# Attention and two feed-forward layers on one core: ScalarE's parametric rectifier carries the sign of a converted weight

## The chip, the cores and the metric

One core of a Trainium2 chip. The metric is device time in microseconds (us); less is better. The engines are TensorE (PE in the rows, its weight loads PEld), VectorE (DVE), ScalarE (ACT), GpSimd (POOL) and SyncE (SP), which here issues the DMAs.

## The reference

Three blocks follow each other, with 2304 tokens of width 512:

```python
# attention: 4 batches, 8 heads, 576 positions, head width 64
scores = q @ k.T / sqrt(64)     # heads 0-3: window of 32; heads 4-7: every 4th of 128 positions
attn = softmax(where(mask, scores, -1e9)) @ v
# first layer, w_in 512x2048, w_out 2048x512
h = x @ w_in
g = (a0 + a1*h + a2*h**2 + a3*h**3) / (1 + |b0|*|h| + |b1|*h**2 + 1e-6)
x = g @ w_out
# second layer, the same sizes
h = x @ w_in
out = (max(h, 0) + alpha * min(h, 0)) @ w_out
```

All four weight matrices reach the chip as 64-bit floats; everything else is 32-bit.

## The kernel before

**Conversion of the weights.** A weight arrives in chunks of 128x512 64-bit floats, seen as pairs of 32-bit words. `w_convert` makes 32-bit floats of two chunks at a time (a 128x1024 tile). The high word holds the sign, eleven bits of exponent and twenty of mantissa. ScalarE reads it as a 32-bit float, takes its absolute value and scales it by 2^-112, which moves the exponent so that its top bits are gone (L377, two instructions of 128x512). VectorE shifts the result left by three bits (L383, one instruction of 128x1024), which pushes them out and makes room for three more mantissa bits. It then ORs in the top three bits of the low word (L393, two instructions of 128x512), and last the sign bit of the high word (L398, two more). For five chunk pairs of the first layer's `w_out`, those in the table `SIGNED`, another way is taken: ScalarE makes the three low bits in place, with a copy on strided 16-bit words (L380, two instructions), and VectorE ORs sign and low bits in together (L386, two instructions). So VectorE has five instructions for a pair outside the table and three for one in it, and ScalarE two and four.

There are 32 such pairs, 16 in each layer. Those of the first layer are converted in the first part of the kernel, where they are also needed first. Of the second layer's, eleven are converted between the first layer's work (`w_early`), stored to DRAM and read back later, and five of `w_out` at the start of the second layer.

**The work on tokens.** `J` counts 48 steps of the first layer; each takes two 128-wide chunks of the hidden width for 384 tokens. A step is an in-projection on TensorE (`inproj`, L618, into the tile `ps_h`, which has two buffers), the rational function on ScalarE and VectorE (`rat_1`, `rat_2`, L636 to L650; L639 is the last instruction that reads a `ps_h` and so the one that frees it), and an out-projection (`outproj1`, L668), which TensorE does two steps later. In the first eight steps the operands are plain 32-bit floats. From the ninth on, each operand is a high and a low part (type fp32r) and each product three matmuls. For that `w_split` makes two parts of every converted weight (L418 on ScalarE, L419 on VectorE), and `g_split` of every result (L657, L658). Every second step also has the scores of an attention unit (L472, L482), its softmax (L494 to L539), its product with v (L553) and the copies of it that the next in-projections read (L583, L588). In this document a pair is two steps with one such unit. The second layer takes its in-projection in seven products of sums (L809) and its out-projection from L687.

**The order of the work.** TensorE, VectorE and ScalarE each run their instructions in the order in which they stand. `in_order_of_need` writes that order at the end of the build: it goes through the recorded instructions with a cost for each and what each depends on, and lets the one with the longest chain behind it go first. It fixes the order of those that it places in its first 197 us (`ORDERED`); behind that the order is that of the tile framework. SyncE's queue has the DMAs in one order: loads of raw weights (L350, L358), of attention (L445, L446), stores of converted weights (L362).

Of the kernel before, what the change touches and what calls it, by code (L numbers as in the profile page):

```python
# [7 lines left out]
F32 = mybir.dt.float32  # L8
# [3 lines left out]
U16 = mybir.dt.uint16  # L12
AF = mybir.ActivationFunctionType
ALU = mybir.AluOpType
# [16 lines left out]
W_BIAS = 2.0 ** -112  # L31
# [9 lines left out]
QW = UB // 2 * HEADS * QB  # L41
KW = UB // 2 * HEADS * CELL
ORDERED = 197e3
SIGNED = (('out', 4), ('out', 6), ('out', 8), ('out', 10), ('out', 12))
WARM = 8
SLOW = 6500
ORDER = "capaaawwwwwwawwwwwwwwa"
# [228 lines left out]
def attn_rational_prelu_kernel(  # L276
# [15 lines left out]
    nc = tc.nc  # L292
    scale = 1.0 / float(D) ** 0.5
# [37 lines left out]
    wt, raw_t, w32_t = {}, {}, {}  # L331
# [21 lines left out]
    def w_early(layer, kind, c):  # L353


        for i in range(2):
            t = rawp.tile([128, 2 * DM], U32, tag="raw", name="raw")
            nc.sync.dma_start(out=t, in_=src[layer, kind][c + i].bitcast(U32))  # L358
            raw_t[layer, kind, c + i] = t
        a = w_convert(layer, kind, c, f"outl{NC - 2}")  # L360
        w_dram[layer, kind, c] = dp.tile([128, 2 * DM], F32, name=f"w_dram_{kind}{c}")
        nc.sync.dma_start(out=w_dram[layer, kind, c], in_=a.bitcast(F32))  # L362

    def w_convert(layer, kind, c, tag=None):


        if layer == 1 or tag:
            a = wp.tile([128, 2 * DM], U32, tag=tag or f"{kind}l{c}", name=f"w{kind}{c}")
        else:
            a = rawp.tile([128, 2 * DM], U32, tag="u", name="u", bufs=1)  # L370
        signed = layer == 1 and (kind, c) in SIGNED
        halves = [slice(i * DM, (i + 1) * DM) for i in range(2)]
        raw = [raw_t.pop((layer, kind, c + i)) for i in range(2)]
        words = [t.rearrange("p (f t) -> p t f", t=2) for t in raw]
        for i in range(2):
            w32_t[layer, kind, c + i] = a[:, halves[i]]
            nc.scalar.activation(out=a[:, halves[i]].bitcast(F32), in_=words[i][:, 1, :].bitcast(F32), func=AF.Abs, scale=W_BIAS)  # L377
            if signed:
                quarters = raw[i].bitcast(U16).rearrange("p (f t) -> p t f", t=4)
                nc.scalar.activation(  # L380
                    out=quarters[:, 2, :], in_=quarters[:, 1, :], func=AF.Copy, scale=2.0 ** -13, bias=-8191.0 / 16384
                )
        nc.vector.tensor_scalar(out=a, in0=a, scalar1=3, scalar2=0, op0=ALU.logical_shift_left, op1=ALU.bitwise_or)  # L383
        if signed:
            for i in range(2):
                nc.vector.scalar_tensor_tensor(  # L386
                    out=a[:, halves[i]], in0=words[i][:, 1, :], scalar=0x80000007, in1=a[:, halves[i]],
                    op0=ALU.bitwise_and, op1=ALU.bitwise_or,
                )
            raw_t[layer, kind, c] = a  # L390
            return a
        for i in range(2):
            nc.vector.scalar_tensor_tensor(  # L393
                out=a[:, halves[i]], in0=words[i][:, 0, :], scalar=29, in1=a[:, halves[i]],
                op0=ALU.logical_shift_right, op1=ALU.bitwise_or,
            )
        for i in range(2):
            nc.vector.scalar_tensor_tensor(  # L398
                out=a[:, halves[i]], in0=words[i][:, 1, :], scalar=0x80000000, in1=a[:, halves[i]],
                op0=ALU.bitwise_and, op1=ALU.bitwise_or,  # L400
            )
        raw_t[layer, kind, c] = a
        return a
# [512 lines left out]
    def w_next(layer):  # L916
        for key in to_convert[layer][:1]:
            while (*key[:2], key[2] + 1) in to_load[layer]:
                w_loads(layer, 1)
            if key not in w_dram:  # L920
                w_convert(*key)
            if layer == 2:
                w_split(*key)
        del to_convert[layer][:1]
# [252 lines left out]
```

## Time and profile before

| | |
|---|---|
| median of three runs | 889.0 us (888.59 to 892.02) |
| the profiled execution | 889.99 us, of which 887.6 us are its span, from the first to the last instruction |
| TensorE | 862.5 us busy, 97% of the span |
| weight loads of TensorE | 765.5 us, 86% |
| VectorE | 761.9 us, 86% |
| ScalarE | 579.5 us, 65% |
| granted clock of TensorE | 0.996 of full speed on average |
| DMA | 90.48 MB, 102 GB/s on average |

The shares are averages over stages that have different limits, and a busy TensorE counts matmuls that overlap, so they are read stage by stage: the first 46 us are the first attention units and the first weights, the first layer ends near 500 us, and the second fills the rest.

### The profile page before, as it was taken

The numbers are of one execution on the slowest core, as the hardware profiler recorded it, in microseconds if no ns is written. First come the engines' busy times: TensorE is split into PE (matmuls) and PEld (weight loads), VectorE is DVE, ScalarE is ACT, GpSimd is POOL, SyncE is SP. The second block draws the span as 40 slices with busy tenths as digits, with TensorE's granted clock in tenths as the row PEclk, the third lists the DMA queues.
The fourth block names the chain that finished last, engine by engine and source line by source line (L and its number), as shares of the span: only waits on it lengthen the run. The fifth ranks groups of instructions, "written<-read, shape, count | busy, mean of one in ns | idle before, by whom it ended". The sixth has DMA issues, their size and how long they took to land.

```text
span 887.6 us, 17356 instructions
## 1 busy us (share of the span) xinstructions
PE 862.5 (97%) x7031; PEld 765.5 (86%) x7032; DVE 761.9 (86%) x1235; ACT 579.5 (65%) x1165; POOL 0.2 (0%) x4
## 2 busy tenths in 40 slices
PE   7899999999999999999999999999999999999998
PEld 5555578889999999898999999898888989899896
DVE  3899999999999899999999999998987678767642
ACT  4699977578777777777677665657554455644423
POOL 0000000000000000000000000000000000000000
PEclk9899999999999999999999999999999999999999
DMA  9956102123333434443021242323220011210001
GB/s 334 356 189 246 38 22 93 38 86 129 130 128 117 159 110 127 163 147 108 18 78 43 76 150 95 119 64 132 87 98 24 25 48 60 95 48 24 1 0 72
DMA packets 32911, 90.48 MB, mean 102 GB/s; under 512 B 3904, under 2 KB 11456, under 8 KB 32832
## 3 DMA queue, kind: packets, MB, share of 16 engines
q1 hardware_dynamic: 32832, 89.38, 29.1%
q8 instruction: 55, 0.90, 0.4%
q14 instruction: 24, 0.20, 0.1%
HBM read 74.17 MB, written 15.20 MB: 101 GB/s over the span
## 4 chain that ended last, share of the span: by engine, by line
PE 61%; DVE 19%; ACT 13%; DMA 4%; issue 2%; SPq 0%; ACTq 0%
PE ps_h L809 19%; PE ps_y L687 14%; PE ps_h L618 9%; PE ps_y L668 9%; PE ps_aS L687 4%; PE ps_aP L687 4%; DVE tc L649 2%; DVE tb L648 2%; ACT p L511 2%; DVE tb L645 2%; ACT tc L637 2%; DVE tc L650 2%; ACT p L526 2%; DVE tc L638 2%; DVE tc L639 2%
## 5 line engine op out<-in xcount | busy, mean ns | idle before, releaser
L618 PE MATMUL ps_h<-xh,winh 128*128 128x384 f32 x320 | 110.2, 344 | 6.8 <-DVE tc L639 6.8
L668 PE MATMUL ps_y<-gh,wouth 128*128 128x384 f32 x320 | 108.0, 338 | 0.0
L668 PE MATMUL ps_y<-gl,wouth 128*128 128x384 f32 x320 | 107.3, 335 | 0.0
L668 PE MATMUL ps_y<-gh,woutl 128*128 128x384 f32 x320 | 107.2, 335 | 0.0
L618 PE MATMUL ps_h<-xh,winl 128*128 128x384 f32 x320 | 107.1, 335 | 0.0
L618 PE MATMUL ps_h<-xl,winh 128*128 128x384 f32 x320 | 107.0, 334 | 0.0
L687 PE MATMUL ps_y<-wouth,gl 128*128 128x512 f32 x192 | 74.9, 390 | 0.0
L687 PE MATMUL ps_y<-woutl,gh 128*128 128x512 f32 x192 | 74.9, 390 | 0.0
L687 PE MATMUL ps_y<-wouth,gh 128*128 128x512 f32 x192 | 74.8, 390 | 0.0
L636 ACT ACTIVATE ta<-ps_h,root 128x384 f32<-128x384 f32 x96 | 56.2, 586 | 26.9 <-PE ps_h L618 22.8
L618 PEld LDWEIGHTS ps_h<-xh,winh 128*128 128x128 f32 x320 | 60.0, 188 | 12.1 <-DVE tc L639 10.5
L637 ACT ACTIVATE tc<-ps_h,co 128x384 f32<-128x384 f32 x96 | 65.3, 680 | 1.4 <-DVE gl L658 1.4
L657 ACT ACTIVATE gh<-tc 128x768 fp32r<-128x768 f32 x40 | 34.1, 851 | 44.2 <-DVE tc L650 44.1
L668 PEld LDWEIGHTS ps_y<-gh,wouth 128*128 128x128 f32 x320 | 60.0, 188 | 0.4
L716 DVE TENSOR_TENSOR gl<-tc,gh 128x768 fp32r<-128x768 f32 x48 | 45.8, 954 | 16.8 <-ACT gh L715 16.7
L715 ACT ACTIVATE gh<-tc 128x768 fp32r<-128x768 f32 x48 | 40.4, 841 | 30.5 <-PE ps_aP L687 28.0
L618 PEld LDWEIGHTS ps_h<-xl,winh 128*128 128x128 f32 x320 | 60.1, 188 | 0.1
L668 PEld LDWEIGHTS ps_y<-gl,wouth 128*128 128x128 f32 x320 | 60.1, 188 | 0.1
L668 PEld LDWEIGHTS ps_y<-gh,woutl 128*128 128x128 f32 x320 | 60.1, 188 | 0.1
L618 PEld LDWEIGHTS ps_h<-xh,winl 128*128 128x128 f32 x320 | 60.1, 188 | 0.0
L715 ACT ACTIVATE st_a<-w 128x1024 fp32r<-128x1024 f32 x24 | 25.5, 1062 | 50.4 <-PE ps_h L809 41.7
L639 DVE SCALAR_TENSOR_TENSOR tc<-tc,co,ps_h 128x384 f32<-128x384 f32 x96 | 58.0, 607 | 0.2
(203 smaller groups left out, 2287.7 us busy)
## 6 DMA issues: line engine op xcount, KB each, us to landing
w<-w_dram_in SPq DMA_DIRECT2D x24, 512.0 KB, 3.3
raw<-in_w_in_dram SPq DMA_DIRECT2D x16, 512.0 KB, 5.2
raw_inh<-in_w_out_dram SPq DMA_DIRECT2D x13, 512.0 KB, 3.4
y_dram<-os SPq DMA_DIRECT2D x24, 192.0 KB, 1.9
out_dram<-os SPq DMA_DIRECT2D x18, 256.0 KB, 2.1
ld_qk<-in_qv_d_dram SPq DMA_DIRECT2D x10, 448.0 KB, 3.5
ld_qk<-in_qv_p_dram SPq DMA_DIRECT2D x10, 416.0 KB, 3.7
raw_inh<-in_w_in_dram SPq DMA_DIRECT2D x8, 512.0 KB, 8.8
```

What stands on the lines that cost most here:

```text
L511: nc.scalar.activation(out=a["p"][:, j * CELL:(j + 1) * CELL], in_=a["s"][p][:, jj * CELL:(jj + 1) * CELL], func=AF.Exp, scale=scale, bias ...
L526: nc.scalar.activation(out=pv, in_=pv, func=AF.Copy, scale=a["rd"][:, j:j + 1])
L618: nc.tensor.matmul(out=hp[:, :BLK], lhsT=w, rhs=x, start=(k == 0), stop=(k == len(pairs) - 1))
L636: nc.scalar.activation(out=ta, in_=hp, func=AF.Abs, scale=root)
L637: nc.scalar.activation(out=tc_, in_=hp, func=AF.Identity, scale=co[:, 3:4], bias=co[:, 2:3])
L639: nc.vector.scalar_tensor_tensor(out=tc_, in0=tc_, scalar=co[:, 1:2], in1=hp, op0=ALU.add, op1=ALU.mult)
L657: nc.scalar.activation(out=hi, in_=g, func=AF.Copy)
L668: nc.tensor.matmul(out=yt[:, :BLK], lhsT=w[:, m * 128:(m + 1) * 128], rhs=g, start=(c == 0 and i == 0), stop=(c == NC - 1 and i == len(pai ...
L687: nc.tensor.matmul(out=yt, lhsT=g[:, tok], rhs=w, start=(first and i == 0), stop=(last and i == 2))
L715: nc.scalar.activation(out=hi, in_=t, func=AF.Copy)
L716: nc.vector.tensor_tensor(out=lo, in0=t, in1=hi.bitcast(F32), op=ALU.subtract)
L809: nc.tensor.matmul(out=hp, lhsT=u[:, ws], rhs=x[:, xs], start=(k == 0), stop=(k == 5))
```

## The change

`w_convert` no longer takes the absolute value. ScalarE's function at this place is the parametric rectifier (`Prelu`), with the scale as before and a slope for negative numbers of -2^32. A positive high word comes out as before. A negative one is made positive too, and 2^32 times as large, so that bit 5 of its exponent field is set; the shift by three that follows puts this bit at the place of the sign. The instructions that ORed in the sign (L398) go, and the table `SIGNED` with its branch (L380, L386). All 32 pairs now have two instructions on ScalarE and three on VectorE.

```diff
--- before.py
+++ after.py
@@ -41,7 +41,7 @@
 QW = UB // 2 * HEADS * QB
 KW = UB // 2 * HEADS * CELL
 ORDERED = 197e3
-SIGNED = (('out', 4), ('out', 6), ('out', 8), ('out', 10), ('out', 12))
+SIGN = -(2.0 ** 32)
 WARM = 8
 SLOW = 6500
 ORDER = "capaaawwwwwwawwwwwwwwa"
@@ -368,36 +368,19 @@
             a = wp.tile([128, 2 * DM], U32, tag=tag or f"{kind}l{c}", name=f"w{kind}{c}")
         else:
             a = rawp.tile([128, 2 * DM], U32, tag="u", name="u", bufs=1)
-        signed = layer == 1 and (kind, c) in SIGNED
         halves = [slice(i * DM, (i + 1) * DM) for i in range(2)]
         raw = [raw_t.pop((layer, kind, c + i)) for i in range(2)]
         words = [t.rearrange("p (f t) -> p t f", t=2) for t in raw]
         for i in range(2):
             w32_t[layer, kind, c + i] = a[:, halves[i]]
-            nc.scalar.activation(out=a[:, halves[i]].bitcast(F32), in_=words[i][:, 1, :].bitcast(F32), func=AF.Abs, scale=W_BIAS)
-            if signed:
-                quarters = raw[i].bitcast(U16).rearrange("p (f t) -> p t f", t=4)
-                nc.scalar.activation(
-                    out=quarters[:, 2, :], in_=quarters[:, 1, :], func=AF.Copy, scale=2.0 ** -13, bias=-8191.0 / 16384
-                )
+            nc.scalar.activation(
+                out=a[:, halves[i]].bitcast(F32), in_=words[i][:, 1, :].bitcast(F32), func=AF.Prelu, scale=W_BIAS, alpha=SIGN
+            )
         nc.vector.tensor_scalar(out=a, in0=a, scalar1=3, scalar2=0, op0=ALU.logical_shift_left, op1=ALU.bitwise_or)
-        if signed:
-            for i in range(2):
-                nc.vector.scalar_tensor_tensor(
-                    out=a[:, halves[i]], in0=words[i][:, 1, :], scalar=0x80000007, in1=a[:, halves[i]],
-                    op0=ALU.bitwise_and, op1=ALU.bitwise_or,
-                )
-            raw_t[layer, kind, c] = a
-            return a
         for i in range(2):
             nc.vector.scalar_tensor_tensor(
                 out=a[:, halves[i]], in0=words[i][:, 0, :], scalar=29, in1=a[:, halves[i]],
                 op0=ALU.logical_shift_right, op1=ALU.bitwise_or,
-            )
-        for i in range(2):
-            nc.vector.scalar_tensor_tensor(
-                out=a[:, halves[i]], in0=words[i][:, 1, :], scalar=0x80000000, in1=a[:, halves[i]],
-                op0=ALU.bitwise_and, op1=ALU.bitwise_or,
             )
         raw_t[layer, kind, c] = a
         return a
```

The lines behind `w_convert` stand 17 lower in the changed kernel (L639 becomes L622, L494 becomes L477). `in_order_of_need` is not edited, but it has other instructions to place, so the order on each engine moves too. Three places follow.

On VectorE, the first step of the first layer: `win` and `wout` are the tiles of converted weights with buffer numbers (`win_465` is the second pair), L638 and L639 the rational function on `ps_h`. Before:

```order
L498 TENSOR_SCALAR nm<-mx 128x6
L398 SCALAR_TENSOR_TENSOR win_465<-raw_outh_153,win_465 128x512
L638 TENSOR_TENSOR tc<-tc,ps_h 128x384
L393 SCALAR_TENSOR_TENSOR wout_569<-raw_inh_155,wout_569 128x512
L639 SCALAR_TENSOR_TENSOR tc<-tc,co,ps_h 128x384
L393 SCALAR_TENSOR_TENSOR wout_569<-raw_outh_157,wout_569 128x512
L519 TENSOR_SCALAR sm<-sm 128x6
L645 SCALAR_TENSOR_TENSOR tb<-ta,ratio 128x768
L520 RECIPROCAL rd<-sm 128x6
L638 TENSOR_TENSOR tc<-tc,ps_h 128x384
L383 TENSOR_SCALAR win_577<-win_577 128x1024
L639 SCALAR_TENSOR_TENSOR tc<-tc,co,ps_h 128x384
```

The same place of the changed kernel:

```order
L381 SCALAR_TENSOR_TENSOR wout_565<-raw_outh_157,wout_565 128x512
L477 TENSOR_REDUCE mx<-ps_aS 128x3
L477 TENSOR_REDUCE mx<-ps_aP 128x3
L621 TENSOR_TENSOR tc<-tc,ps_h 128x384
L481 TENSOR_SCALAR nm<-mx 128x6
L622 SCALAR_TENSOR_TENSOR tc<-tc,co,ps_h 128x384
L502 TENSOR_SCALAR sm<-sm 128x6
L503 RECIPROCAL rd<-sm 128x6
L628 SCALAR_TENSOR_TENSOR tb<-ta,ratio 128x768
L522 STREAM_TRANSPOSE pts<-p 128x384
L621 TENSOR_TENSOR tc<-tc,ps_h 128x384
L622 SCALAR_TENSOR_TENSOR tc<-tc,co,ps_h 128x384
```

The first `wout` is now whole before the step begins, and no conversion stands between L621 and L622 (before: L638 and L639).

On ScalarE, the stage in which the first layer's weights are converted, from a copy of an attention unit (L583) on. Before:

```order
L583 ACTIVATE xh_788<-ps_aS 128x192
L583 ACTIVATE xh_788<-ps_aP 128x192
L380 ACTIVATE raw_inh_175<-raw_inh_175 128x512
L380 ACTIVATE raw_outh_177<-raw_outh_177 128x512
L377 ACTIVATE win_1005<-raw_inh_877 128x512
L377 ACTIVATE win_1005<-raw_outh_879 128x512
L377 ACTIVATE wout_927<-raw_inh_776 128x512
L377 ACTIVATE wout_927<-raw_outh_778 128x512
L380 ACTIVATE raw_inh_776<-raw_inh_776 128x512
L380 ACTIVATE raw_outh_778<-raw_outh_778 128x512
L636 ACTIVATE ta<-ps_h,root 128x384
L637 ACTIVATE tc<-ps_h,co 128x384
```

The changed kernel there:

```order
L566 ACTIVATE xh_778<-ps_aS 128x192
L566 ACTIVATE xh_778<-ps_aP 128x192
L376 ACTIVATE win_987<-raw_inh_863 128x512
L376 ACTIVATE win_987<-raw_outh_865 128x512
L376 ACTIVATE wout_911<-raw_inh_766 128x512
L376 ACTIVATE wout_911<-raw_outh_768 128x512
L376 ACTIVATE wout_993<-raw_inh_867 128x512
L376 ACTIVATE wout_993<-raw_outh_869 128x512
L376 ACTIVATE win_1125<-raw_inh_960 128x512
L376 ACTIVATE win_1125<-raw_outh_962 128x512
L629 ACTIVATE ta<-tb,c1t 128x768
L619 ACTIVATE ta<-ps_h,root 128x384
```

The four copies of 16-bit words are gone, and two more pairs are converted in their place.

On VectorE, a conversion of `w_early` (the third pair of the second layer's `w_out`) between two steps, with buffer numbers, of which those of `ps_h` tell the in-projections apart. Before:

```order
L638 TENSOR_TENSOR tc_4069<-tc_4069,ps_h_4083 128x384
L519 TENSOR_SCALAR sm_4097<-sm_4097 128x6
L398 SCALAR_TENSOR_TENSOR wout4_4331<-raw_4327,wout4_4331 128x512
L639 SCALAR_TENSOR_TENSOR tc_4069<-tc_4069,co_109,ps_h_4083 128x384
L520 RECIPROCAL rd_4112<-sm_4097 128x6
L648 SCALAR_TENSOR_TENSOR tb_4068<-tb_4068,ta_4067 128x768
L649 SCALAR_TENSOR_TENSOR tc_4069<-tc_4069,co_109,ta_4067 128x768
L539 STREAM_TRANSPOSE pts_4127<-p_4096 128x384
L650 SCALAR_TENSOR_TENSOR tc_4069<-tb_4068,tc_4069 128x768
L638 TENSOR_TENSOR tc_4159<-tc_4159,ps_h_4160 128x384
L398 SCALAR_TENSOR_TENSOR wout4_4331<-raw_4329,wout4_4331 128x512
L639 SCALAR_TENSOR_TENSOR tc_4159<-tc_4159,co_109,ps_h_4160 128x384
```

The changed kernel, the last two instructions of the same conversion:

```order
L381 SCALAR_TENSOR_TENSOR wout4_4289<-raw_4285,wout4_4289 128x512
L481 TENSOR_SCALAR nm_4009<-mx_4008 128x6
L641 TENSOR_TENSOR gl_4199<-tc_3847,gh_4198 128x768
L621 TENSOR_TENSOR tc_4027<-tc_4027,ps_h_4028 128x384
L381 SCALAR_TENSOR_TENSOR wout4_4289<-raw_4287,wout4_4289 128x512
L622 SCALAR_TENSOR_TENSOR tc_4027<-tc_4027,co_109,ps_h_4028 128x384
L502 TENSOR_SCALAR sm_4055<-sm_4055 128x6
L503 RECIPROCAL rd_4070<-sm_4055 128x6
L628 SCALAR_TENSOR_TENSOR tb_4026<-ta_4025,ratio_111 128x768
L621 TENSOR_TENSOR tc_4027<-tc_4027,ps_h_4041 128x384
L622 SCALAR_TENSOR_TENSOR tc_4027<-tc_4027,co_109,ps_h_4041 128x384
```

Where a sign instruction stood in front of L639 twice, no instruction of the conversion is left; the conversion ends one step earlier.

## Rows read from the trace of the kernel before

**Rows 1.** Busy time by stage: start:end, length, then each engine's busy us (instructions).

```profile
core 0: us, PE busy (x) PEld busy (x) DVE busy (x) ACT busy (x) POOL busy (x), PEclk, DMA share, GB/s
27.70:46.41 18.71, 15.81 (x200) 8.56 (x197) 15.88 (x32) 14.23 (x40) 0.00 (x0) 0.89 0.88 341
46.41:127.87 81.46, 80.77 (x728) 49.62 (x728) 79.84 (x140) 76.95 (x167) 0.00 (x0) 1.00 0.36 126
127.87:190.92 63.05, 59.02 (x643) 53.64 (x637) 60.13 (x94) 42.06 (x107) 0.00 (x0) 1.00 0.18 57
190.92:209.67 18.75, 18.75 (x215) 18.11 (x209) 18.48 (x32) 14.03 (x36) 0.00 (x0) 1.00 0.27 93
209.67:406.54 196.87, 191.54 (x2186) 182.39 (x2181) 183.82 (x313) 149.50 (x375) 0.00 (x0) 1.00 0.41 136
500.36:610.00 109.64, 109.64 (x565) 100.78 (x565) 105.35 (x164) 65.04 (x87) 0.00 (x0) 1.00 0.29 97
610.00:660.00 50.00, 49.43 (x248) 44.12 (x247) 44.85 (x71) 29.68 (x41) 0.00 (x0) 1.00 0.34 110
```

**Rows 2.** The same view for the in-projections (L618) alone: PE, PEld.

```profile
127.87:190.92 63.05, 26.64 (x144) 24.75 (x145) 1.00 0.18 57
209.67:406.54 196.87, 88.80 (x480) 82.59 (x481) 1.00 0.41 136
```

**Rows 3.** Who waited for whom, whole span: us in total, times, longest.

```profile
PE ps_h L618 <- DVE tc L639: 9.9, 13, 1.9
...
ACT win L377 <- DMA raw<-in_w_in_dram: 3.8, 3, 3.1
...
ACT win L377 <- DMA w_dram_in<-win: 2.7, 2, 1.8
```

**Rows 4.** Timeline of VectorE near 316 us: start, length, engine, line, operation.

```profile
315.76 0.56 DVE L638 TENSOR_TENSOR tc<-tc,ps_h 128x384 f32<-128x384 f32 x1
...
316.30 0.69 DVE L398 SCALAR_TENSOR_TENSOR wout<-raw,wout 128x512 uint32<-128x512 uint32 x1
316.91 0.61 DVE L639 SCALAR_TENSOR_TENSOR tc<-tc,co,ps_h 128x384 f32<-128x384 f32 x1
```

**Rows 5.** Busy time by stage of the sign instructions (L398) alone, on VectorE.

```profile
27.70:46.41 18.71, 2.63 (x4) 0.89 0.88 341
46.41:127.87 81.46, 9.61 (x14) 1.00 0.36 126
127.87:190.92 63.05, 1.36 (x2) 1.00 0.18 57
...
209.67:406.54 196.87, 13.33 (x20) 1.00 0.41 136
...
500.36:610.00 109.64, 6.51 (x10) 1.00 0.29 97
```

**Rows 6.** L398 over the whole span, then L380 over the whole span.

```profile
0.00:887.60 887.60, 36.05 (x54) 1.00 0.30 102
...
0.00:887.60 887.60, 12.79 (x10) 1.00 0.30 102
```

**Rows 7.** Groups of instructions, shapes apart: busy us, mean ns, then idle before.

```profile
L377 ACT ACTIVATE wout<-raw_inh 128x512 f32<-128x512 f32 x8 | 5.7, 713 | 0.0
...
L380 ACT ACTIVATE raw_outh<-raw_outh 128x512 uint16<-128x512 uint16 x5 | 7.4, 1474 | 0.0
```

**Rows 8.** Busy time in the second stage of ScalarE's absolute values (L377) alone.

```profile
46.41:127.87 81.46, 13.21 (x21) 1.00 0.36 126
```

**Rows 9.** TensorE's first in-projections in the timeline, then the clock around them (view of Rows 1).

```profile
27.70 4.16 PE L618 MATMUL ps_h<-xh,win 128*128 128x384 f32 x6
...
32.45 3.49 PE L618 MATMUL ps_h<-xh,win 128*128 128x384 f32 x10
...
28.00:32.00 4.00, 4.00 (x32) 1.76 (x38) 2.06 (x4) 1.32 (x4) 0.00 (x0) 0.54 1.03 405
```

**Rows 10.** The line L929, instructions: duration in ns (min/median/max), starts.

```profile
L929 ACT ACT_TABLE_LOAD  x1: 1283/1283/1283, 0.7 to 0.7; - x1
```

## The prediction

> **What bounds the kernel now.** I read the busy time by stage first, because the shares of the whole span hide the limits. In the first layer TensorE runs one pair (two steps and an attention unit) after the other. From 190.92 to 209.67 us one pair runs with TensorE busy for all of its 18.75 us, and VectorE is busy for 18.48 us of them [rows 1]. I take 18.75 us as the shortest time of a pair of the later kind; that VectorE is 98.6% busy in it without holding TensorE up says that VectorE does no harm as long as its work fits.
>
> In-projections count the pairs: 48 of them make one, so the stretch from 127.87 to 190.92 us holds 3 (144) and that from 209.67 to 406.54 us holds 10 (480) [rows 2]. Three pairs at 18.75 us are 56.25 us; the stretch takes 63.05 us, 6.8 us more. Ten are 187.5 us; the stretch takes 196.87 us, 9.4 us more. VectorE is busy for 60.13 and 183.82 us there, 95% and 93% [rows 1]. In the waits, what TensorE waits for is above all L639 on VectorE, which frees `ps_h`: 9.9 us in 13 waits [rows 3]. And the timeline shows a sign instruction (L398) of 0.69 us standing between L638 and L639 [rows 4], so it delays the freeing by its own length. So here the first layer ends late because VectorE has a little too much to do, in the wrong places.
>
> From 46.41 to 127.87 us TensorE is busy for 80.77 of 81.46 us, though VectorE (79.84) and ScalarE (76.95) are nearly full as well [rows 1]: all three are at their limit, and TensorE alone sets the pace. In the second layer TensorE is full to 610 us and misses 0.57 us in the next 50 us [rows 1].
>
> **What the change removes.** On VectorE, the 54 sign instructions, 36.05 us in all [rows 6]: 27 pairs outside the table with two each. (The five signed pairs keep three instructions: L386 becomes L381.) On ScalarE, the ten strided copies, 12.79 us [rows 6]. It adds nothing to either. By stage the sign instructions are 2.63, 9.61, 1.36, 13.33 and 6.51 us [rows 5]; two more lie ahead of these stretches, and two behind the fourth.
>
> **The price of the rectifier.** No row shows one. Its nearest row is the instruction it takes the place of: the same tile, stride, scale and engine, 713 ns in one group; at the other end stands the strided copy of the same 512 columns, 1474 ns [rows 7]. Nothing suggests less than the first, and I take the first, so no change on ScalarE. The Trainium skill ("ScalarE: Activation LUTs", What ACT_TABLE_LOAD costs) gives the same rate for every function and 186 ns + 0.833 ns per column with immediate operands; by that it would be an estimated 613 ns, whatever the function; the rows are dearer than that for the absolute value already, and by either price no term of the sum changes.
>
> **The sum, stage by stage.**
>
> 27.70 to 46.41 us: TensorE is idle for 2.9 of 18.71 us [rows 1]. The order shows that no conversion is left between the instructions that free `ps_h` in the first step, and 2.63 us leave VectorE. But the DMA is 88% busy here [rows 1], and weights that have not come can't be converted. I take half: 1.5 us, between 0 and 2.9. The first six matmuls take 4.16 us where ten later ones take 3.49, with the clock at 0.54 on average [rows 9]; I leave these 2.1 us (4.16 less six tenths of 3.49) as they are, since the attention units ahead of them hardly move.
>
> 46.41 to 127.87 us: 9.61 us leave VectorE and 12.79 us ScalarE, but TensorE can gain only its idle 0.7 us. I take 0.7. What VectorE saves is hidden behind TensorE; its use is that VectorE enters the next stage without arrears.
>
> 127.87 to 190.92 us: only 1.36 us of sign instructions lie here, and the splits of the weights (L419), which the change keeps, fill this stage. With all else in place VectorE would need 60.13 - 1.36 = 58.8 us, more than the 56.25 us of TensorE. So VectorE stays the bound here, and what helps beyond 1.4 us are its arrears. The order moves a split or two ahead; most stay. I take a stage of 59 us, a gain of 4.0, between 1.4 and 6.8.
>
> 209.67 to 406.54 us: VectorE needs 183.82 - 13.33 = 170.5 us, 91% of the 187.5 us that TensorE needs, well below the 98.6% that did no harm. And no conversion stands in front of L639 any more in the place shown. What may stay are ScalarE's waits for the raw loads and for the store of the converted tile, 3.8 and 2.7 us [rows 3]; the store leaves when the conversion's last instruction is done, and the next raw loads stand behind it in SyncE's queue, so an earlier end starts both earlier. If these 6.5 us stayed in full on TensorE's path, the gain would be 9.4 - 6.5 = 2.9. I take 7.5, between 2.9 and 9.4.
>
> 500 us and after: 6.51 us leave VectorE, whose work is covered by TensorE, full to 610 us. I take 0.3 of the 0.57 us behind it.
>
> Sum: 1.5 + 0.7 + 4.0 + 7.5 + 0.3 = 14.0 us. The profiled execution took 889.99 us, which gives 876.0; it lies 1.0 us above the median of 889.0, so I predict **875 us**. The lower bounds sum to 0 + 0 + 1.4 + 2.9 + 0 = 4.3 us (884.7), the upper ones to 2.9 + 0.7 + 6.8 + 9.4 + 0.6 = 20.4 us (868.6), and 2.1 us more if the half clock at the start went too (866.5).
>
> **The rivals.**
>
> *TensorE's limit is reached.* Every wait of the first layer goes: 868.6 us, down to 866.5. For it: VectorE's 91% in the long stage. Against it: VectorE's 58.8 us in the split stage. Chance 0.07 for anything below 870.
>
> *A dear rectifier: no gain.* If it costs what the strided copy does, 1474 ns, each is 0.76 us dearer. In the second stage 21 of them [rows 8] bring 16 us for the 12.79 that go, so ScalarE is where it was, at its limit; in the long stage each conversion holds ScalarE 1.5 us longer, about the 1.3 us that VectorE gives up for it, so TensorE's waits move from L639 to ScalarE's instructions ahead of it. Only the arrears of the split stage are left: some 2 us, 887 us. For it: ScalarE too was full when VectorE was. Against it: only the function differs. Chance, with any other way in which the waits merely change hands (the raw loads, for one): 0.11.
>
> *Table loads: slower.* The Trainium skill ("ScalarE: Activation LUTs", Table sets: the hidden batching unit) says that cheap functions stand in every table set and names relu, copy, identity and abs; it doesn't name the parametric one. As a mechanism of this kernel: the trace has one table load of 1283 ns, at the start [rows 10]. If the rectifier were not in the loaded table, each conversion would need one before and one after, 2.57 us. In the second stage ScalarE has 81.46 - 76.95 = 4.5 us free and gains 12.79, so from the seventh conversion on it would be late; the stage has about ten (21 instructions [rows 8]), 26 us, so some 9 us late, and in the long stage ten times 2.57 us come in place of 13.33 us on VectorE and eat the gain. 889 + 9 = 898 us. Against it: the changed program's order on ScalarE has no load beside the first. Chance 0.05, with any order that turns out worse by as much.
>
> **How the numbers follow.** The forecast, a gain between 4.5 and 19 us, has the rest, 0.77. A measurement of this kernel tells 0.5%, 4.4 us, from no change. Faster than 884.6: 0.77 + 0.07 = 0.84; the same 0.11; slower 0.05. The range goes from 866 us, the limit of TensorE with the clock, to 885 us, the sum of the lower bounds; some 0.16 lie outside it.
>
> **What would show it.** Right: the rectifier at 0.65 to 0.72 us; 54 instructions fewer on VectorE; the ten pairs at under 19.0 us each; TensorE's waits for L622 (L639 before) at a third or less; the three pairs with the splits still above 18.75 us. Wrong: a rectifier above 1 us; more than one table load; pairs of the long stage still near 19.7 us, with TensorE waiting for something else, the raw loads above all; or a split stage as long as before, if VectorE had no arrears when it began.

## The result and the profile after

The changed kernel takes 881.21 us (median of four runs, 880.1 to 882.98); the kernel before took 889.7 us beside it (median of four, 888.59 to 892.02). The ratio is 0.9903, with a 95% interval from 0.9875 to 0.9931. So the kernel is faster by 8.5 us, within the range of the prediction and 6 us short of its number, 875. The profiled execution of the changed kernel took 882.98 us, of which 881.2 us are its span.

The page of the changed kernel begins so (busy time of each engine, share of the span, instructions):

```profile
span 881.2 us, 17303 instructions
PE 861.2 (98%) x7031; PEld 765.8 (87%) x7032; DVE 734.2 (83%) x1181; ACT 568.9 (65%) x1155; POOL 0.2 (0%) x4
```

VectorE has 1181 instructions, where the page of before shows 1235; that is the 54 that were to go. Its busy time fell by 27.7 us, less than the 36.05 us of [rows 6]; that figure counts each instruction in full, while the records of neighbours overlap (in [rows 4] L639 begins 0.08 us before L398 ends). ScalarE's busy time fell by 10.6 us, and TensorE's idle time (the span less its busy time) from 25.1 to 20.0 us.

The same stages as in [rows 1], with the ends that they now have, answer where the time came from (start:end, length, busy us of each engine with its instructions, granted clock, DMA share, GB/s):

```profile
core 0: us, PE busy (x) PEld busy (x) DVE busy (x) ACT busy (x) POOL busy (x), PEclk, DMA share, GB/s
29.88:47.73 17.85, 15.32 (x197) 8.64 (x196) 13.43 (x26) 14.55 (x40) 0.00 (x0) 0.94 0.90 343
47.73:127.79 80.06, 80.06 (x729) 49.76 (x729) 78.95 (x135) 70.47 (x161) 0.00 (x0) 1.00 0.34 122
127.79:185.23 57.44, 57.44 (x642) 53.43 (x636) 55.51 (x88) 39.96 (x104) 0.00 (x0) 1.00 0.23 74
185.23:203.96 18.73, 18.73 (x216) 18.10 (x209) 17.97 (x32) 14.16 (x36) 0.00 (x0) 1.00 0.25 85
203.96:398.84 194.88, 190.75 (x2186) 181.90 (x2181) 171.31 (x290) 146.26 (x373) 0.00 (x0) 1.00 0.40 137
398.84:418.88 20.04, 18.34 (x166) 17.73 (x161) 16.91 (x29) 14.47 (x36) 0.00 (x0) 1.00 0.23 75
```

Read against [rows 1], stage by stage: the first stage takes 17.85 us for 18.71, the second 80.06 for 81.46, the three pairs with the splits 57.44 for 63.05, the next pair 18.73 for 18.75, the ten pairs of the long stage 194.88 for 196.87. The pair behind them takes 20.04 us; in the trace of before it took 18.94 (406.54 to 425.48 us), so 1.1 of the 2.0 us are given back there. The first in-projection begins at 29.88 us instead of 27.70, and what follows these stages is 0.2 us longer. Sum: -2.2 + 0.9 + 1.4 + 5.6 + 0.0 + 2.0 - 1.1 - 0.2 = 6.4 us, the difference of the two spans (887.6 and 881.2). The 2.2 us at the start are taken up under the hardware; without them the stages give 8.6 us, close to the 8.5 us of the medians.

The long stage is the surprise. VectorE is busy for 12.5 us less than before and TensorE still idles for 4.1 us in it, where it idled for 5.3. These are waits of that stage (engine and line that waited, for whom; us in total, times, longest):

```profile
ACT gh L640 <- DVE tc L633: 27.9, 13, 4.2
DVE tb L631 <- ACT ta L630: 12.2, 13, 1.5
...
PE ps_h L601 <- DVE tc L622: 3.7, 6, 1.0
```

The same waits in the kernel before, in its long stage (209.67 to 406.54 us):

```profile
ACT gh L657 <- DVE tc L650: 21.2, 9, 3.9
...
DVE tb L648 <- ACT ta L647: 5.1, 9, 1.8
...
PE ps_h L618 <- DVE tc L639: 3.2, 5, 0.9
```

TensorE still waits for the instruction that frees `ps_h` (L622). Over the whole span that is 6.7 us in 8 waits, where [rows 3] has 9.9 in 13, but in this stage it is 3.7 us for 3.2: the sign instructions are gone, and the wait is not shorter. Above it ScalarE waits for VectorE and VectorE for ScalarE, 28 and 12 us, where it was 21 and 5: L640, the high part of a step's result, waits for the end of the rational function (L633). So 7.1 us of what left VectorE are now spent in its longer wait for ScalarE. How the two engines hold each other shows in one place of the stage. First the chain of work there (start us, us, what), then VectorE's timeline and one row of TensorE's (start, length, engine, line, operation, in brackets the idle time before it and who ended it):

```profile
281.60 2.94 DMA w_dram_in<-win
...
284.61 0.68 ACT wout L376
285.29 0.47 ACT ta L619
285.76 1.77 ACT p L494 x12
287.53 0.48 ACT tc L620
```

```profile
287.56 0.17 DVE L502 TENSOR_SCALAR sm<-sm 128x6 f32<-128x6 f32 x1 [2.02 <-ACT p L494]
...
288.13 0.55 DVE L621 TENSOR_TENSOR tc<-tc,ps_h 128x384 f32<-128x384 f32 x1 [0.17 <-ACT tc L620]
288.60 1.02 DVE L628 SCALAR_TENSOR_TENSOR tb<-ta,ratio 128x768 f32<-128x768 f32 x1
289.53 0.61 DVE L622 SCALAR_TENSOR_TENSOR tc<-tc,co,ps_h 128x384 f32<-128x384 f32 x1
```

```profile
290.20 0.44 PE L601 MATMUL ps_h<-xh,winh 128*128 128x384 f32 x1 [0.97 <-DVE tc L622]
```

A conversion waits on ScalarE for the store of the tile that it writes to (a DMA of 2.94 us). Behind it stand L619, then the six exponentials of the softmax (L494, 1.77 us), and only then the L620 that VectorE's L621 needs. VectorE, which has been idle for 2.02 us until the exponentials end, then does L628, a later part of the step, between L621 and L622. When L622 is done, TensorE has stood for 0.97 us. No sign instruction is left in this place. What makes L622 late here is the order in which the two queues hold their instructions.

### The profile page after: what moved, and what is told of

It reads as the page before. It is cut to its first block, busy times and chain, and to the rows that moved or that the text cites. A ratio compares the mean times of both kernels' runs of the same rounds, so it can differ in the third digit from the quotient of the medians.

```text
span 881.2 us, 17303 instructions
## 1 busy us (share of the span) xinstructions
PE 861.2 (98%) x7031; PEld 765.8 (87%) x7032; DVE 734.2 (83%) x1181; ACT 568.9 (65%) x1155; POOL 0.2 (0%) x4
## 4 chain that ended last, share of the span: by engine, by line
PE 72%; DVE 13%; ACT 9%; DMA 3%; issue 3%; SPq 0%; ACTq 0%; DVEq 0%
PE ps_h L792 19%; PE ps_y L670 14%; PE ps_y L651 14%; PE ps_h L601 14%; PE ps_aS L670 4%; PE ps_aP L670 4%; ACT p L494 2%; DVE tc L632 2%; DVE tc L633 2%; ACT p L509 1%; DVE tb L631 1%; DMA w_dram_in<-win 1%; DVE tc L622 1%; DVE tc L621 1%; DVE tb L628 1%
## 5 line engine op out<-in xcount | busy, mean ns | idle before, releaser
L619 ACT ACTIVATE ta<-ps_h,root 128x384 f32<-128x384 f32 x96 | 56.2, 586 | 32.7 <-PE ps_h L601 32.4
L620 ACT ACTIVATE tc<-ps_h,co 128x384 f32<-128x384 f32 x96 | 65.1, 680 | 0.0
L640 ACT ACTIVATE gh<-tc 128x768 fp32r<-128x768 f32 x40 | 34.3, 857 | 43.8 <-DVE tc L633 43.7
L699 DVE TENSOR_TENSOR gl<-tc,gh 128x768 fp32r<-128x768 f32 x48 | 45.8, 955 | 16.6 <-ACT gh L698 16.4
L629 ACT ACTIVATE ta<-tb,c1t 128x768 f32<-128x768 f32 x48 | 45.4, 945 | 21.9 <-DVE tb L628 21.9
L631 DVE SCALAR_TENSOR_TENSOR tb<-tb,ta 128x768 f32<-128x768 f32 x48 | 45.8, 955 | 15.3 <-ACT ta L630 14.9
```

The source lines that it names most:

```text
L619: nc.scalar.activation(out=ta, in_=hp, func=AF.Abs, scale=root)
L620: nc.scalar.activation(out=tc_, in_=hp, func=AF.Identity, scale=co[:, 3:4], bias=co[:, 2:3])
L629: nc.scalar.activation(out=ta, in_=tb, func=AF.Ln, bias=c1t)
L631: nc.vector.scalar_tensor_tensor(out=tb, in0=tb, scalar=C1, in1=ta, op0=ALU.add, op1=ALU.mult)
L640: nc.scalar.activation(out=hi, in_=g, func=AF.Copy)
L699: nc.vector.tensor_tensor(out=lo, in0=t, in1=hi.bitcast(F32), op=ALU.subtract)
```

## The experiments

Two theories were set against each other for the long stage. **Load**: VectorE still has too much to do. **Place**: ScalarE's and VectorE's instructions stand in an order in which each waits for the other, whatever the load. Each median below is beside runs of the kernel before on the same chip (889.1 to 889.7 us).

### The new conversion in one layer only

`w_convert` is kept in both forms and chosen by layer. The first experiment has the new one in the first layer, the second in the second:

```diff
+    def w_convert(layer, kind, c, tag=None):
+        return (w_convert_new if layer == 1 else w_convert_old)(layer, kind, c, tag)
```

> The rectifier for the first layer's 16 conversions alone; the second layer's keep absolute value and sign instructions. Theory P (place: the long stage is held by ScalarE's queue and the two-way dependence of ScalarE and VectorE, not by VectorE's load): nearly all of the gain of 8.5 us is here, 6 to 8.5 us, so about 882 us; the first pair behind the splits starts some 5.5 us earlier than before. Theory L (load: every microsecond that leaves VectorE counts): 6 us at most, since only 15 of the 36 us of sign instructions go, so 883.5 us or more.

> The rectifier for the second layer's 16 conversions alone. Theory P: 0 to 2.5 us faster than before, 887 to 889.5 us, and the ten pairs of the long stage take 194 to 197 us. Theory L: 13.3 us leave VectorE in the long stage, so 5 us or more faster, 884 us or less, and the ten pairs take 191 us or less.

New in the first layer alone: 881.01 us, ratio 0.9903 (0.9890 to 0.9917), as much as the whole change, as the theory of place expected. New in the second alone: 888.87 us, 0.9989 (0.9981 to 0.9998), 0.1%, also as that theory expected. The split stage and the long stage of the first:

```profile
126.47:183.86 57.39, 57.39 (x642) 53.38 (x636) 55.51 (x88) 39.94 (x104) 0.00 (x0) 1.00 0.22 73
202.61:398.69 196.08, 191.72 (x2186) 182.33 (x2181) 180.97 (x309) 148.26 (x374) 0.00 (x0) 1.00 0.42 141
```

and of the second:

```profile
127.01:190.07 63.06, 58.97 (x641) 53.60 (x637) 60.16 (x94) 42.06 (x107) 0.00 (x0) 1.00 0.18 59
208.79:403.33 194.54, 190.80 (x2186) 181.82 (x2180) 172.93 (x293) 146.71 (x374) 0.00 (x0) 1.00 0.41 138
```

The gain of the split stage (63.1 to 57.4 us) comes with the five signed and eleven other pairs of the first layer, and no bit of it with the second's. The conversions that lie in the long stage are the second layer's; taking their sign instructions out frees VectorE of 10.9 us there (183.82 to 172.93) and shortens the stage by 2.3 us, of which the end shows 0.9. By my step of the long stage (7.5 us for 13.33) it would have been 6.1 us.

### The eleven early conversions without VectorE, and without any engine

The next two take load out of the long stage altogether. In the first, the early conversions return after ScalarE's part, so VectorE's shift and ORs are left out. In the second nothing is converted: the raw loads arrive unread, and one tile of zeros is stored eleven times.

```diff
+        if tag:
+            raw_t[layer, kind, c] = a
+            return a
```

```diff
-        a = w_convert(layer, kind, c, f"outl{NC - 2}")
+        for i in range(2):
+            raw_t.pop((layer, kind, c + i))
+        if not blank:
+            blank.append(wp.tile([128, 2 * DM], F32, tag=f"outl{NC - 2}", name="blank"))
+            nc.vector.memset(blank[0], 0.0)
+        a = blank[0]
```

> The changed kernel, with VectorE's whole part (three instructions) left out of the eleven conversions between the first layer's steps, so that the second layer's weights are wrong; another 20 us leave VectorE. Theory P: the long stage keeps most of what it has above 187.5 us; 0 to 3 us faster than the changed kernel (878 to 881 us). Theory L: 5 us or more faster than the changed kernel (876 us or less), the ten pairs at 189 us or less.

> The changed kernel without ScalarE's and VectorE's part of those eleven conversions: the raw loads stay, and zeros are stored in place of the converted weights, so the output is wrong. It shows what the stage takes when nothing of a conversion stands in either queue. Theory P: the ten pairs fall to 188 to 190 us, 4 us or more below the run without VectorE's part; 873 to 876 us. Theory L: within 1.5 us of the run without VectorE's part, since VectorE's load is the same. If the stage stays above 192 us here too, neither holds: the loss is then in the attention units and the steps themselves.

Without VectorE's part: 883.8 us, 0.9929 (0.9914 to 0.9945), if anything slower than the changed kernel (0.9903, with intervals that overlap), where both theories had expected it to be faster. Its long stage, and ScalarE's waits in it for the stores (the profiled execution took 887.31 us, the longest of the four):

```profile
203.12:404.99 201.87, 191.99 (x2186) 182.51 (x2180) 158.40 (x262) 148.78 (x374) 0.00 (x0) 1.00 0.41 140
```

```profile
ACT win L376 <- DMA w_dram_out<-wout: 5.3, 2, 4.3
ACT win L376 <- DMA w_dram_in<-win: 5.1, 2, 3.8
```

Without any conversion: 878.53 us, 0.9877 (0.9864 to 0.9891). Its long stage, and the two longest waits in it:

```profile
203.01:396.13 193.12, 189.76 (x2187) 182.21 (x2181) 158.35 (x262) 138.01 (x354) 0.00 (x0) 1.00 0.43 146
```

```profile
ACT gh L647 <- DVE tc L640: 34.1, 16, 3.2
DVE tb L638 <- ACT ta L637: 12.8, 19, 1.4
```

This speaks against load: VectorE is busy for 82% of the stage and ScalarE for 71%, no rectifier and no sign instruction is in it, and it still takes 193.12 us, 5.6 above the 187.5 of ten pairs. It hurts place as I had it, too: I had put the wait at the conversions, and without them only 1.8 of 194.88 us go. The wait of `gh` for the end of the rational function (L647 and L640 here) is even longer than with them. So the loss lies in the steps and attention units themselves, as the last sentence of the expectation has it; that it is their order is tested below. The first of the two kernels agrees from the other side: 13 us of VectorE's work less, and the stage is 7 us longer in the profiled execution. ScalarE waits 10.4 us for the stores there; that this is the reason is not shown.

### Two tiles for the early conversions

The store wait by itself: the early conversions write to two tiles in turn. The room for the second comes from narrower attention buffers.

```diff
-        a = w_convert(layer, kind, c, f"outl{NC - 2}")
+        n_early.append(c)
+        a = w_convert(layer, kind, c, f"outl{NC - 2}" if len(n_early) % 2 else "cv2")
```

> The changed kernel with two tiles in turn for the converted weights of the eleven early conversions (the attention buffers made narrower to find the room), so that ScalarE need not wait for the store of the last one. If the store wait is what holds the long stage, its two waits of 2.6 us go and the stage with them: 4 us or more faster, 877 us or less. If the order on ScalarE holds it: 0 to 3 us faster, 878 to 881 us.

880.55 us, 0.9890 (0.9872 to 0.9908); the long stage takes 194.35 us. ScalarE's two waits for the store (5.3 us in the changed kernel) are gone, and TensorE's waits for L622 in the stage (here L626) fall from 3.7 to 2.2 us:

```profile
PE ps_h L605 <- DVE tc L626: 2.2, 6, 0.6
```

So what the chain above shows at its head was worth 0.5 us of the stage, and the median can't tell it from nothing: the store wait doesn't hold the stage.

### The written order carried further

`ORDERED` ends the written order at 197 us of its own reckoning; from there on the tile framework's order stands, and the long stage lies behind that point but for its beginning: the traces of the changed kernel and of the one with the order to 385 part on ScalarE at 214 us and on VectorE at 219 us of the changed kernel's time, where the stage begins at 203.96. One number is changed, on the changed kernel to 430e3, 410e3, 385e3 and 360e3:

```diff
-ORDERED = 197e3
+ORDERED = 385e3
```

> The changed kernel with ORDERED at 430e3 in place of 197e3, so that the planner's order holds through the whole long stage (it puts the exponentials on ScalarE between the instructions of a step, where the tile framework's order has all of them ahead of it). If the order on ScalarE is what holds the long stage: the ten pairs at 188 to 191 us, 4 us or more faster than the changed kernel, 877 us or less. If it is the store wait or VectorE's load: within 1.5 us of it, 879.5 to 882.5 us.

> The changed kernel with ORDERED at 410e3. With 430e3 the ten pairs ran at TensorE's limit, but behind the planner's region five instructions that prepare the second layer stood ahead of a step's last ones on VectorE, and TensorE waited 4.8 us. If that wait belongs to the place where the planner's order ends, another end changes it while the long stage keeps 188 to 190 us: 875 to 879 us where the wait goes, near 881 us where it stays.

> The same with 385e3: the last pair or two are back in the tile framework's order, so the long stage at 188 to 191 us. 875 to 879 us where the wait at the end of the order goes, near 881 us where it stays.

> The same with 360e3: the last two or three pairs in the tile framework's order, the long stage at 189 to 192 us, and the end of the order 70 us ahead of the second layer, so that the wait there is least likely: 876 to 879 us.

| order to | median us (range) | ratio (95%) |
|---|---|---|
| 197 (the change) | 881.21 (880.1 to 882.98) | 0.9903 (0.9875 to 0.9931) |
| 360 | 876.84 (875.8 to 877.6) | 0.9861 (0.9846 to 0.9877) |
| 385 | 874.28 (872.68 to 875.09) | 0.9831 (0.9815 to 0.9847) |
| 410 | 882.87 (881.39 to 883.14) | 0.9930 (0.9916 to 0.9944) |
| 430 | 881.02 (879.41 to 882.19) | 0.9902 (0.9889 to 0.9916) |

The long stage and the eleven steps behind it, up to the end of the first layer, with the order to 385:

```profile
201.18:389.52 188.34, 188.34 (x2188) 182.01 (x2181) 167.34 (x282) 145.82 (x368) 0.00 (x0) 1.00 0.31 110
389.52:483.60 94.08, 93.95 (x602) 93.25 (x597) 90.94 (x131) 67.05 (x116) 0.00 (x0) 1.00 0.35 123
```

and two waits in its long stage, the longest and the one for `gh`:

```profile
ACT ta L619 <- PE ps_h L601: 26.9, 19, 3.1
...
ACT gh L640 <- DVE tc L633: 0.9, 2, 0.5
```

TensorE is busy for the whole of the long stage, 18.83 us a pair. ScalarE hardly waits for `gh` any more (0.9 us for 27.9 in the changed kernel); what it waits for is TensorE, 26.9 us. That is how a stage reads in which TensorE sets the pace: the others wait for it. The number of conversions is not quite the same, since the longer order moves three of the ten behind the stage (14 rectifiers instead of 20 in it), but the kernel with none at all took 193.12 us, so their number is not what does it. The edit also moves DMAs in SyncE's queue, while TensorE's projections keep their order through the stage. The DMAs are hardly the cause, since with the two tiles ScalarE waits only 0.9 us for raw loads and not at all for stores, and the stage still takes 194.35 us; but no run changed the order on ScalarE and VectorE alone.

The run with 430 was to take 877 us or less if the order holds the stage. Its median of 881.02 us misses that, while its long stage of 188.19 us is as expected. Why 410 and 430 give the gain back shows for 430 in the eleven steps behind the stage:

```profile
201.11:389.30 188.19, 188.19 (x2188) 181.84 (x2181) 167.34 (x282) 145.76 (x368) 0.00 (x0) 1.00 0.31 110
389.30:490.25 100.95, 94.96 (x597) 93.89 (x593) 92.17 (x132) 67.11 (x115) 0.00 (x0) 0.98 0.32 110
```

The long stage is as short, and 6.9 us are lost behind it. The chain there (start us, us, what):

```profile
473.36 0.87 DVE st_B21l L699
...
476.03 0.88 DVE gl L641
476.91 0.04 issue
476.95 5.14 PE ps_y L651 x20
482.09 4.16 PE ps_h L601 x24
486.25 4.16 PE ps_y L651 x24
```

TensorE waits 4.8 us for `gl` (L641), the low part of a step's result, which stands on VectorE behind the preparations of the second layer (`st_B21l` and others of L699). The wait changes with the place where the written order ends: 4.8 us at 430, 5.7 at 410, 0.5 at 385 and 1.4 at 360.

With both edits, two tiles and the order to 430, the kernel takes 882.5 us, 0.9914 (0.9900 to 0.9928). The same wait for `gl` is there again with 4.8 us, so the second tile doesn't help at that place.

> Both of the last two edits. If they are two separate losses the gains add up: 873 to 876 us. If the order is all of it: within 1.5 us of the run with the longer order alone.

### The longer order without the change

Was the order alone enough? The kernel before got the same edit, to 430 and to 385.

> The kernel before with ORDERED at 430e3. If the order on ScalarE holds the long stage by itself, the kernel before gains as much from it as the changed one does, 4 us or more, with its sign instructions in place (885 us or less). If VectorE's load becomes the limit once the order is good, it gains 0 to 2 us, and the rectifier is then worth more than it was: 10 us or more between this run and the changed kernel with the longer order.

> The kernel before with ORDERED at 385e3, the end at which the changed kernel ran in 874.3 us. If order and rectifier are separate gains, the longer order gives the kernel before some 7 us too, so 882 to 883 us. If VectorE's load decides once the order is good, the sign instructions keep it from that: 886 us or more, and the rectifier is worth 12 us or more with this order, against 8.5 without it.

It was not: 895.61 us, 1.0070 (1.0053 to 1.0086), and 897.74 us, 1.0105 (1.0087 to 1.0123), both slower than before, which no expectation for 430 had. With the order to 385, its long stage and the eleven steps behind it:

```profile
210.55:404.22 193.67, 189.66 (x2187) 181.97 (x2181) 176.31 (x299) 147.33 (x369) 0.00 (x0) 1.00 0.34 118
404.22:508.29 104.07, 96.45 (x598) 93.92 (x593) 96.75 (x141) 68.77 (x118) 0.00 (x0) 0.98 0.31 104
```

Its long stage gets 3.2 us shorter than in [rows 1], and behind it TensorE loses 10.0 us against the changed kernel with the same number (104.07 and 94.08). With the order to 385 the change is worth 897.74 - 874.28 = 23.5 us. Of the spans, 9.4 us come up to the long stage (it begins at 210.55 and 201.18 us; 0.9 of that is a later first in-projection), 5.3 in it and 10.0 behind it. TensorE's longest waits in the stage, and then those behind it:

```profile
PE ps_y L668 <- ACT os L674: 1.9, 1, 1.9
PE ps_aS L472 <- DVE xl L588: 1.6, 1, 1.6
```

```profile
PE ps_y L668 <- DVE gl L658: 4.7, 2, 3.9
PE ps_h L618 <- DVE tc L639: 2.9, 5, 0.8
```

In the stage these are `os` on ScalarE and `xl` on VectorE, and none is L639. Behind it the longest wait is again the one for `gl`, which stands on VectorE behind preparations of the second layer (L716, L733), as in the changed kernel with the order to 430. So a good part of the 23.5 us is the place where the written order ends, and the same number ends it at another place in a kernel with other instructions. With the order to 430 both kernels have that wait with 4.8 us, and the change is worth 895.61 - 881.02 = 14.6 us, 6.1 more than the 8.5 with the short order. VectorE's load (176.31 us in the long stage with the order to 385, and 167.34 us in the changed kernel) and the 2.9 us for L639 fit that. But the two kernels differ in their order as well, so it is not shown that the load does it.

## Why the prediction was right or wrong

**The rectifier's price: right.** Eight of the 64 rectifiers and the only table load (count, duration ns min/median/max, first and last start):

```profile
L376 ACT ACTIVATE wout<-raw_inh x8: 658/673/781, 29.7 to 81.3; 128x512 f32<-128x512 f32 x8
L912 ACT ACT_TABLE_LOAD  x1: 1283/1283/1283, 0.7 to 0.7; - x1
```

It costs about what the absolute value did (a mean of 713 ns in [rows 7]), not the 1474 ns of the strided copy, and it stands in the loaded table. Both rivals that rested on it, no gain and slower, fall; what the first of them names beside it, waits that merely change hands, is what the long stage came to. The Trainium skill ("ScalarE: Activation LUTs", What ACT_TABLE_LOAD costs) says that the rate is the same for every function, and the rows of the two functions lie close together (a median of 673 ns here); the estimate of 613 ns worked out from that page for this shape is 60 ns below the median here.

**27.70 to 46.41 us (1.5 predicted, 0.9 measured): right in kind.** The stage is shorter, DMA is still 90% busy, and TensorE is still idle for 2.5 us.

**46.41 to 127.87 us (0.7 predicted, 1.4 measured): right in kind, above its bound.** TensorE has no idle time left in it. The stage even fell 0.7 us below its former busy time, so the busy time of overlapping matmuls was not quite the floor that I took it for.

**The split stage (4.0 predicted, 5.6 measured): right about the arrears, wrong about the bound.** I let VectorE keep 58.8 us of work there and stay the bound. It kept 55.51, 4.6 us less than before, though only 1.36 us of sign instructions lay there. Two of the stage's twelve splits (L419, 2.4 us) went ahead, into the stage where VectorE had got free; that is the "split or two" that the prediction named, but its 58.8 us still held them. With that TensorE became the limit: it is busy for all of the 57.44 us. That the first layer's conversions alone do all of it is shown by the first experiment (57.39 us).

**The long stage (7.5 predicted, 2.0 measured, 0.9 with the pair behind it): the step that failed.** I compared VectorE's 170.5 us with TensorE's 187.5, found 91%, and took from a pair with 98.6% that a share below that does no harm. VectorE's 171.31 us came out as reckoned; what follows from them did not. A pair takes 19.49 us, not under 19.0. I had also put the 9.9 us that TensorE waits for L639 beside the 9.4 us of this stage, but [rows 3] is of the whole span; 3.2 us of the waits lie in this stage, and they became 3.7. The pair with 98.6% lies where the order is written; nearly all of the long stage lies behind the end of it, where ScalarE and VectorE wait for each other for 28 and 12 us at shares of 75% and 88%. The share of busy time says nothing about that. The sign instruction between L638 and L639 in [rows 4] was a true delay, but not the one that set the stage. My lower bound of 2.9 us, from the store and the raw loads, named a wrong cause as well: the store is worth 0.5 us. Shown: load isn't it (193.12 us with VectorE 82% busy and no conversion, 188.34 us with it 89% busy in another order), the store isn't it, and with another order the loss is gone (188.2 to 188.3 us). Not settled: which element of the order does it. The six exponentials ahead of L620, the place of L628 ahead of L622 and the place of `gh` all move together when the order changes, and no run moved one alone.

**After 500 us (0.3 predicted, -0.2 measured): nothing, as the 0.1% of the second experiment shows.**

The sum: the stages gave 8.6 us where it had 14.0. The long stage brought 5.5 too little and the pair behind it took 1.1 back, the first stage brought 0.6 too little and the end 0.5, the second 0.7 and the split stage 1.6 too much. The miss is the long stage. That the time still lies in the range doesn't bear that step out: the range was wide enough to hold without it, and the stage's own lower bound of 2.9 us was missed.

## What to carry to other kernels

A busy share near the top doesn't by itself say that an engine is the limit, and one well below doesn't say that it is harmless: two engines with in-order queues that feed each other can hold a third up at 75% and 88%, and the row to look for is the pair of long waits in both directions. Leave the suspected work out altogether before you cost its removal; here one kernel without the early conversions showed that 5.6 us would stay. Where an order is written by hand or by a planner up to some point, look at both sides of that point: freed time is only worth something where the order can use it, and the best version here, 874.28 us, is the change and the longer order together, while the longer order alone, at the two ends tried, made the kernel slower.

## What the runs showed of the hardware

In three places of these traces TensorE's granted clock was low right behind a stretch in which it had waited, and so the wait cost more than its length. With the order to 430 TensorE waits 4.8 us for `gl`. The 20 matmuls behind that wait take 5.14 us in the chain above, where 24 of them take 4.16 a few microseconds later, so 20 would take 3.47; 1.7 us go to the clock. The 4.8 and the 1.7 us are nearly all of the 6.9 us that this kernel loses behind the long stage (100.95 and 94.08 us). The mean granted clock around it:

```profile
470.00:490.25 20.25, 15.45 (x81) 15.13 (x80) 20.25 (x29) 11.70 (x18) 0.00 (x0) 0.92 0.36 116
```

In the kernel before with the order to 385, 20 such matmuls behind the wait of 3.9 us for `gl` take 5.28 us (granted clock 0.83 from 480 to 490 us). The same is seen at the start of the changed kernel:

```profile
24.00:28.00 4.00, 1.99 (x52) 1.36 (x44) 3.03 (x6) 1.02 (x3) 0.00 (x0) 0.67 1.01 404
28.00:32.00 4.00, 4.00 (x70) 3.03 (x71) 2.15 (x4) 3.44 (x8) 0.00 (x0) 0.50 1.03 409
```

TensorE is idle for 2.0 us between 24 and 28 us; from 28 to 32 us it is busy throughout and is granted 0.50, the lower of its two levels (1.2 and 2.4 GHz). In the traces of the changed kernel and of the one with the order to 385, ScalarE and VectorE have the same instructions in the same order up to 211 us, and yet the first in-projection began at 26.7 us (order to 385) and at 29.9 us (the changed kernel). So I don't put the 2.2 us of the later start down to the change; what decides between an early and a late start stays open.
